# Gathered top bytes moved from a tile of their own into the tile of the joined words

## The chip, the cores and the metric

One Trainium2 chip, one of its cores. The metric is the device time of one execution of the program in microseconds (us); differences are taken between medians of several executions.

## The reference

For 8 batches of 576 rows, the kernel computes linear attention for 8 heads of 64, an RMS norm, and a mixing and feed-forward part. Cut to what matters:

```python
kv  = einsum('bhsd,bhse->bhde', k, v)
out = einsum('bhsd,bhde->bhse', q, kv)
x   = out / sqrt(mean(out * out, axis=-1) + 1e-6) * g_norm   # heads side by side: (8, 576, 512)
u   = x + ((x.T @ U) @ V).T                                  # along the sequence, rank 32
y   = u + maximum(u @ w_ch1, 0) @ w_ch2                      # 512 -> 2048 -> 512
```

All values are float32, except U, V, w_ch1 and w_ch2, which arrive as 64-bit floating-point words and have to be joined to 32-bit words on the chip.

## The kernel before, in words

**Names.** P is 128 partitions, DM is 512, a pair is two heads, a piece f (0 to 15) is 128 columns of w_ch1 with the 128 matching rows of w_ch2, a block j (0 to 8) is 512 rows of the 4608.

**Weights.** `load_w` brings piece f as 64-bit words (1 MB) into a weight slot; SyncE (SP) issues the loads. `decode_w` turns it into float32 and splits it into a high and a low part, `ws`, in the same slot. Piece 0 is decoded in two halves, w1 and w2, by `decode_first`, with parts of the tile `temps` as the target; pieces 1 to 15 take the tile `dec`, of which the pool holds two, so that pieces of equal parity share one. `decode_bytes` has seven steps for a piece:

- line 104, ScalarE (ACT): the gather, byte 4 of every 8-byte word into the tile `packed`, first part (b)
- lines 105, 106, 107 and 109, VectorE (DVE): four operations on these bytes, from b into the second part (c), four bytes to a 32-bit word
- line 111, ACT: c, byte by byte, into the top bytes of the tile `top`
- line 112, DVE: the low words, shifted, are joined with `top` into `temps` or `dec`

Then ACT casts the joined words to the high part (line 117 in `split`, line 125 for the halves), and DVE subtracts it for the low part (line 118, or 137). There is one `packed` and one `top`.

**Attention.** For each batch and pair: `kv_step` (lines 241, 245, and the copies into `kvb`, line 125), `out_step` (lines 264 to 268), `stats_step` (280 to 286), `mul_step` (293, 295), `xsplit_step`, `turn_step`, `t_step` (333, 336), `t4_step` (for the first batch the cast of line 125 on ACT or 131 on DVE, and the subtraction of line 347 on DVE, both into a tile that is called `st` for pairs 1 to 3), and the mix. For the first batch the mix is `mix_first` (matmuls of line 378 before them as fill, 387) and `mix_rest` (396, 398, line 127 into `ut`, then the casts of line 117 into `uth` and the subtractions of line 118 into `utl`).

**Feed-forward.** For each block j and piece f: `ffn1` (lines 414 to 416, three matmuls for each of four column groups), `relu` (line 423 on ACT gives hh, line 424 on DVE gives hl), and `ffn2` of the piece before (line 431). During block 0 `decode_w` runs two pieces ahead; during blocks 0 to 6 the attention of the next batch is woven in.

**Order.** The source is written in the order of a table (`PLAN`); a scheduler that lays the work out by its own estimate then sets the order on each engine, with the tiles' buffers as limits. Each engine works through its own order, and an instruction whose inputs or buffers are not free holds those behind it.

Of the kernel before, what the change touches and what calls it, by code (L numbers as in the profile page):

```python
# [14 lines left out]
U32 = mybir.dt.uint32  # L15
# [5 lines left out]
DM, DF, R = 512, 2048, 32  # L21
P = 128
# [26 lines left out]
def build(ctx: ExitStack, tc: tile.TileContext, kv_in, kvt0_in, kvt_in, q_in, uv_in, g_in, w_in, out):  # L49
# [6 lines left out]
    sc = ctx.enter_context(tc.tile_pool(name="sc", bufs=1))  # L56
    st = ctx.enter_context(tc.tile_pool(name="st", bufs=3))
    dec = ctx.enter_context(tc.tile_pool(name="dec", bufs=2))
    pk = ctx.enter_context(tc.tile_pool(name="pk", bufs=1))
    sm = ctx.enter_context(tc.tile_pool(name="sm", bufs=2))  # L60
    ps_y = ctx.enter_context(tc.tile_pool(name="ps_y", bufs=4, space=bass.MemoryType.PSUM))
    ps_h = ctx.enter_context(tc.tile_pool(name="ps_h", bufs=1, space=bass.MemoryType.PSUM))
# [11 lines left out]
    def weight_slot(name, shape, dtype, f):  # L74

        return const.tile(shape, dtype, name=name, tag=f"w_{f}")
# [18 lines left out]
    def decode_bytes(raw, tmp, top):  # L95

        n = tmp.shape[-1]
        words = raw.bitcast(U32).rearrange("p (n t) -> p n t", t=2)  # L100
        ends = raw.bitcast(U8).rearrange("p (n t) -> p n t", t=8)[:, :, 4]
        packed = pk.tile([P, 2, DM // 2], U32, name="packed")
        b, c = packed[:, 0, 0:n // 4], packed[:, 1, 0:n // 4]
        nc.scalar.copy(out=b.bitcast(U8), in_=ends)
        nc.vector.tensor_scalar(out=c, in0=b, scalar1=0x7f7f7f7f, scalar2=None, op0=ALU.bitwise_and)
        nc.vector.tensor_scalar(out=c.bitcast(U8), in0=c.bitcast(U8), scalar1=56.0, scalar2=71.0, op0=ALU.max, op1=ALU.min)
        nc.vector.tensor_scalar(out=c, in0=c, scalar1=3, scalar2=0x38383838,
                                op0=ALU.logical_shift_left, op1=ALU.bitwise_and)
        nc.vector.scalar_tensor_tensor(out=c, in0=b, scalar=0xC0C0C0C0, in1=c,
                                       op0=ALU.bitwise_and, op1=ALU.bitwise_or)  # L110
        nc.scalar.copy(out=top[:, 0:n].bitcast(U8).rearrange("p (n t) -> p n t", t=4)[:, :, 3], in_=c.bitcast(U8))  # L111
        nc.vector.scalar_tensor_tensor(out=tmp.bitcast(U32), in0=words[:, :, 0], scalar=5, in1=top[:, 0:n],
                                       op0=ALU.logical_shift_right, op1=ALU.bitwise_or)

    def split(hi, lo, src, lo_eng):

        nc.scalar.copy(out=hi, in_=src)
        lo_eng.tensor_tensor(out=lo, in0=src, in1=hi.bitcast(F32), op=ALU.subtract)

    def move(which, n, out, in_, mul=None):  # L120

        e = ENG[which][n]
        if e == "a":
            if mul is None:
                nc.scalar.copy(out=out, in_=in_)
            else:
                nc.scalar.mul(out=out, in_=in_, mul=mul)
        else:
            eng = nc.vector if e == "v" else nc.gpsimd
            if mul is None:  # L130
                eng.tensor_copy(out=out, in_=in_)
            else:
                eng.tensor_scalar(out=out, in0=in_, scalar1=mul, scalar2=None, op0=ALU.mult)

    def minus(which, n, out, in0, in1):
        eng = nc.vector if ENG[which][n] == "v" else nc.gpsimd
        eng.tensor_tensor(out=out, in0=in0, in1=in1, op=ALU.subtract)
# [36 lines left out]
    raws, w1s, w2s = {}, {}, {}  # L174
# [16 lines left out]
    def keep(which, f, hi, lo):  # L191
        w_sb[which][f] = [t.rearrange("p (d c) -> p d c", c=P) for t in (hi, lo)]

    def decode_first(which, tmp, n):
        decode_bytes(raws.pop(which), tmp, tops[n % 1])
        w = const.tile([P, 2, DM], F32R, name=f"{which}s0", tag=f"{which}_0")
        move("wh", n, w[:, 0], tmp)
        minus("wl", n, w[:, 1], tmp, w[:, 0].bitcast(F32))
        keep(which, 0, w[:, 0], w[:, 1])

    def decode_w(f):

        tmp = dec.tile([P, 2 * DM], F32, name="dec")
        decode_bytes(raws.pop(f), tmp, tops[f % 1])
        w = weight_slot(f"ws{f}", [P, 2, 2, DM], F32R, f)
        t = tmp.rearrange("p (w c) -> p w c", w=2)
        split(w[:, 0], w[:, 1], t, nc.vector)
        for n, which in enumerate(("w1", "w2")):
            keep(which, f, w[:, 0, n], w[:, 1, n])
# [245 lines left out]
    tops = [const.tile([P, 2 * DM], U32, name=f"top{n}") for n in range(1)]  # L455
# [73 lines left out]
    for p in range(NPAIR):  # L529
# [5 lines left out]
        tasks.append((PLAN["pair"][p] + PLAN["mt"][p], lambda p=p: mix_rest(p)))  # L535
    ahead = 1
    tasks.append((PLAN["w0"], lambda: decode_first("w1", early[0], 0)))
    tasks.append((PLAN["x0"], lambda: decode_first("w2", early[1], 2)))
    for _, what in sorted(tasks, key=lambda t: t[0]):
        what()  # L540
# [39 lines left out]
    for j in range(NBLK):  # L580
        todo = prep_schedule(j + 1)
        y = None
        for f in range(NF):
            if j == 0:
                while ahead < min(NF, f + 1 + AHEAD):
                    decode_w(ahead)
                    ahead += 1
            end = False
            if j == 0 and f < NEARLY:
                h = hs[f]  # L590
                ffn1(h, f, [3], j)
            else:
                end = j == NBLK - 1 and f == NF - 1
                h = ps_p.tile([P, BLK], F32, name="pp") if end else ps_h.tile([P, BLK], F32, name="h")
                ffn1(h, f, range(ND), j)
            hcur = (f, *relu(h, end))
            for w in todo.get(2 * f, []):
                w()
            if hprev is not None and not (j == NBLK - 1 and f > NF - 3):
                ffn2(y_prev if f == 0 else y, [hprev])  # L600
            if f == 0:
                if j > 0:
                    finish(y_prev, j - 1)
                y = outputs(j)
            for w in todo.get(2 * f + 1, []):
                w()
            held = (held + [hcur])[-3:]
            hprev = hcur
        y_prev = y
# [58 lines left out]
```

## Time and profile before

| | |
|---|---|
| median of 3 executions | 927.5 us (926.78 to 928.56) |
| the profiled execution, its own time | 928.11 us |
| its span, first to last instruction | 926.3 us |
| busy: TensorE (PE), DVE, ACT, POOL | 910.5, 412.2, 281.0, 49.1 us |
| mean granted clock of PE | 0.994 of the full one |
| PE in the first of 40 slices of the span | 7 tenths busy, 9 or more from the third on |

Times in the rows count from the start of the span. A row of the timeline has the start and the length of a record; the brackets behind it say how long the engine was idle before it and what ended that.

### The profile page before, as it was taken

How to read it: one execution, taken by the hardware profiler on the slowest of the kernel's cores; microseconds unless marked ns; L12 is line 12 of the kernel's file. 1: busy time of each engine (PE TensorE's matmuls, PEld its weight loads, DVE VectorE, ACT ScalarE, POOL GpSimd, SP SyncE). 2: the span in 40 equal slices, each digit the busy share in tenths (PEclk: the TensorE clock that was granted, in tenths of full speed). 3: DMA queues.
4: the chain of work that ended last, by engine and by line, in shares of the span. 5: the costliest groups of instructions: out<-in, count | busy, mean ns of one | idle time of the engine just before them, and what ended most of it. 6: DMA issues, size and time to landing. Idle time of an engine off the chain costs nothing.

```text
span 926.3 us, 12207 instructions
## 1 busy us (share of the span) xinstructions
PE 910.5 (98%) x4570; PEld 763.4 (82%) x4570; DVE 412.2 (44%) x885; ACT 281.0 (30%) x587; POOL 49.1 (5%) x68
## 2 busy tenths in 40 slices
PE   7799999999999999999999999999999999999998
PEld 6678888888888888888888888888788888888887
DVE  5988896443354435434344445434344331112112
ACT  5677773222232222222222222222222121111110
POOL 3000002000020002000200010000200020002000
PEclk9899999999999999999999999999999999999999
DMA  9952213121132122212121112212111010001001
GB/s 344 418 217 71 68 57 90 64 68 44 47 101 59 28 77 81 69 32 76 51 61 55 55 57 64 83 31 72 59 49 27 13 46 1 1 1 45 1 1 46
DMA packets 42875, 65.48 MB, mean 71 GB/s; under 512 B 9664, under 2 KB 27840, under 8 KB 42816
## 3 DMA queue, kind: packets, MB, share of 16 engines
q1 hardware_dynamic: 42816, 64.70, 21.2%
q8 instruction: 36, 0.59, 0.3%
q14 instruction: 23, 0.19, 0.1%
HBM read 46.97 MB, written 9.44 MB: 61 GB/s over the span
## 4 chain that ended last, share of the span: by engine, by line
PE 94%; DVE 3%; DMA 1%; ACT 1%; issue 0%; POOL 0%; SPq 0%; DVEq 0%; POOLq 0%
PE y L431 40%; PE h L414 14%; PE h L415 14%; PE h L416 14%; PE pp L241 3%; PE pp L264 3%; PE pp L336 1%; DMA w1raw<-w_in 1%; PE pp L406 1%; PE pp L338 1%; PE pp L266 1%; PE pp L431 1%; DVE utl L372 0%; ACT top L111 0%; DMA out<-st 0%
## 5 line engine op out<-in xcount | busy, mean ns | idle before, releaser
L431 PE MATMUL y<-hh,ws 128*128 128x512 f32 (+1 forms) x1072 | 351.1, 394 | 0.0
L424 DVE SCALAR_TENSOR_TENSOR hl<-h,hh 128x512 fp32r<-128x512 f32 x142 | 97.9, 689 | 301.3 <-ACT hh L423 299.9
L431 PEld LDWEIGHTS y<-hh,ws 128*128 128x128 f32 x1072 | 194.1, 188 | 36.2 <-ACT hh L423 0.6
L414 PE MATMUL h<-uth,ws 128*128 128x512 f32 x536 | 211.7, 395 | 1.3 <-DVE hl L424 1.3
L415 PE MATMUL h<-utl,ws 128*128 128x512 f32 x536 | 210.1, 392 | 0.0
L416 PE MATMUL h<-uth,ws 128*128 128x512 f32 x536 | 209.6, 391 | 0.0
L431 PE MATMUL y<-hl,ws 128*128 128x512 f32 (+1 forms) x536 | 207.2, 387 | 0.0
L423 ACT ACTIVATE hh<-h 128x512 fp32r<-128x512 f32 x142 | 84.8, 597 | 389.9 <-PE h L416 389.6
L414 PEld LDWEIGHTS h<-uth,ws 128*128 128x128 f32 x536 | 101.1, 189 | 24.8 <-DVE hl L424 3.0
L416 PEld LDWEIGHTS h<-uth,ws 128*128 128x128 f32 x536 | 101.1, 189 | 21.9
L431 PEld LDWEIGHTS y<-hl,ws 128*128 128x128 f32 x536 | 100.6, 188 | 20.7
L415 PEld LDWEIGHTS h<-utl,ws 128*128 128x128 f32 x536 | 101.1, 189 | 20.1
L443 POOL TENSOR_TENSOR st<-st,utl 128x512 f32<-128x512 f32 x32 | 40.6, 1290 | 784.7 <-DVE st L442 781.4
L408 DVE TENSOR_TENSOR ut<-pp,ut 128x288 f32<-128x288 f32 x56 | 24.9, 456 | 46.0 <-DMA ut<-xt 32.4
L442 DVE TENSOR_TENSOR st<-y,uth 128x512 f32<-128x512 f32 x32 | 21.3, 686 | 45.7 <-PE y L431 32.1
L371 ACT ACTIVATE uth<-ut,g_sb 128x448 fp32r<-128x448 f32 (+7 forms) x56 | 27.6, 530 | 44.1 <-DVE ut L408 35.1
L280 DVE TENSOR_REDUCE sums<-x 128x10 f32<-128x640 f32 x32 | 26.1, 817 | 24.4 <-ACT x L268 24.4
L372 DVE SCALAR_TENSOR_TENSOR utl<-ut,g_sb,uth 128x448 fp32r<-128x448 f32 (+7 forms) x56 | 26.9, 513 | 11.8 <-ACT uth L371 6.5
L241 PE MATMUL pp<-kv_sb 128*128 128x128 f32 x232 | 31.5, 274 | 0.0
L241 PEld LDWEIGHTS pp<-kv_sb 128*128 128x128 f32 x232 | 29.5, 191 | 1.1
L264 PE MATMUL pp<-kvb,q_sb 128*128 128x128 f32 x224 | 29.5, 274 | 0.0
L264 PEld LDWEIGHTS pp<-kvb,q_sb 128*128 128x128 f32 x224 | 28.3, 191 | 0.8
(202 smaller groups left out, 779.7 us busy)
## 6 DMA issues: line engine op xcount, KB each, us to landing
raw<-w_in SPq DMA_DIRECT2D x15, 1023.6 KB, 14.8
kv_sb<-kv_in SPq DMA_DIRECT2D x29, 512.0 KB, 3.5
q_sb<-q_in SPq DMA_DIRECT2D x29, 288.0 KB, 2.9
out<-st SPq DMA_DIRECT2D x32, 256.0 KB, 2.0
ut<-xt SPq DMA_DIRECT2D x224, 20.0 KB, 1.8
ut<-xt SPq DMA_DIRECT2D x224, 16.0 KB, 1.8
kvt_sb<-kvt_in SPq DMA_DIRECT2D x27, 128.0 KB, 3.1
kvq<-kv_in SPq DMA_DIRECT2D x3, 512.0 KB, 9.4
```

The lines of the kernel that those rows point to most:

```text
L241: nc.tensor.matmul(pp[:, 0:P], lhsT=m[:, i * P:(i + 1) * P], rhs=m[:, MAIN + i * P:MAIN + (i + 1) * P], start=(i == 0 and b < NATIVE), sto ...
L264: nc.tensor.matmul(big[:, i * P:(i + 1) * P], lhsT=qt[:, TAIL + i * P:TAIL + (i + 1) * P], rhs=kb, start=True, stop=True)
L280: nc.vector.tensor_reduce(out=sums.rearrange("p (i h) -> p i h", h=2), in_=xv, axis=AX.X, op=ALU.add)
L371: nc.scalar.mul(out=hi, in_=src, mul=g_sb)
L372: nc.vector.scalar_tensor_tensor(out=lo, in0=src, scalar=g_sb, in1=hi.bitcast(F32), op0=ALU.mult, op1=ALU.subtract)
L414: nc.tensor.matmul(h, lhsT=w1s[f][0][:, d, :], rhs=uh[:, d, :], start=(d == 0), stop=False)
L415: nc.tensor.matmul(h, lhsT=w1s[f][0][:, d, :], rhs=ul[:, d, :], start=False, stop=False)
L416: nc.tensor.matmul(h, lhsT=w1s[f][1][:, d, :], rhs=uh[:, d, :], start=False, stop=(d == ND - 1))
L423: nc.scalar.activation(out=hh, in_=h, func=AF.Relu)
L424: nc.vector.scalar_tensor_tensor(out=hl, in0=h, scalar=0.0, in1=hh.bitcast(F32), op0=ALU.max, op1=ALU.subtract)
L431: nc.tensor.matmul(acc, lhsT=w2s[f][w][:, c, :], rhs=h[:, cols], start=(f == 0 and w == 0 and h is hh), stop=(f == NF - 1 and w == 1))
L443: nc.gpsimd.tensor_tensor(out=o, in0=o, in1=ul[:, c, :].bitcast(F32), op=ALU.add)
```

## The change

The pool `pk` and its tile `packed` are gone. The bytes b and what is made of them, c, now lie in the first and second quarter of `tmp`, the tile that line 112 writes at the end: `temps` for the two halves of piece 0, one of the two `dec` tiles for the others. The two other lines name the one tile `top` directly, and change nothing.

```diff
@@ build
-    pk = ctx.enter_context(tc.tile_pool(name="pk", bufs=1))
@@ decode_bytes
-        packed = pk.tile([P, 2, DM // 2], U32, name="packed")
-        b, c = packed[:, 0, 0:n // 4], packed[:, 1, 0:n // 4]
+        b, c = [tmp[:, i * n // 4:(i + 1) * n // 4].bitcast(U32) for i in range(2)]
@@ decode_first
-        decode_bytes(raws.pop(which), tmp, tops[n % 1])
+        decode_bytes(raws.pop(which), tmp, tops[0])
@@ decode_w
-        decode_bytes(raws.pop(f), tmp, tops[f % 1])
+        decode_bytes(raws.pop(f), tmp, tops[0])
```

The numbers of the later lines fall by two (line 104 of before is line 102 of the change, 112 is 110, 378 is 376). With other buffers the scheduler also lays the instructions out in another order. PE's order is the same up to the first matmuls of line 431; SP's is the same for its first 33 loads. Three places where ACT's and DVE's differ:

ACT, around the cast into `st` for pair 3 of the first batch, before (rawN and wsN belong to piece N):

```order
L127 ACTIVATE ut32_2_94<-y_514,g_sb_97 128x64
L117 CAST uth_569<-ut32_1_93 128x64
L117 CAST uth_569<-ut32_2_94 128x64
L111 COPY top0_103<-packed_547 128x1024
L125 CAST st_141<-y_449 64x128
L104 COPY packed_590<-raw3_174 128x1024
L117 CAST ws2_555<-dec_546 128x1024
```

and in the change:

```order
L115 CAST ws2_548<-dec_540 128x1024
L102 COPY dec_669<-raw4_179 128x1024
L109 COPY top0_100<-dec_582 128x1024
L125 ACTIVATE ut32_0_89<-y_481,g_sb_94 128x64
L125 ACTIVATE ut32_1_90<-y_485,g_sb_94 128x64
L125 ACTIVATE ut32_2_91<-y_509,g_sb_94 128x64
L115 CAST uth_562<-ut32_0_89 128x64
L115 CAST uth_562<-ut32_1_90 128x64
L115 CAST uth_562<-ut32_2_91 128x64
L123 CAST st_138<-y_446 64x128
```

The gather of piece 3, which stood behind the cast into `st`, has moved ahead of these rows, and the gather of piece 4 stands at the top, behind the cast of piece 2 and ahead of everything for pair 3.

DVE, the same place, from the last byte operation of piece 2 to the subtraction into `st`, before:

```order
L109 SCALAR_TENSOR_TENSOR packed_547<-packed_547 128x256
L118 TENSOR_TENSOR utl_570<-ut32_0_92,uth_569 128x64
L118 TENSOR_TENSOR utl_570<-ut32_1_93,uth_569 128x64
L118 TENSOR_TENSOR utl_570<-ut32_2_94,uth_569 128x64
L112 SCALAR_TENSOR_TENSOR dec_546<-raw2_172,top0_103 128x1024
L347 TENSOR_TENSOR st_141<-y_449,st_141 64x128
```

and in the change, from the subtraction that gives the low part of piece 2:

```order
L116 TENSOR_TENSOR ws2_548<-dec_540,ws2_548 128x1024
L105 TENSOR_SCALAR dec_582<-dec_582 128x256
L107 SCALAR_TENSOR_TENSOR dec_582<-dec_582 128x256
L103 TENSOR_SCALAR dec_669<-dec_669 128x256
L104 TENSOR_SCALAR dec_669<-dec_669 128x1024
L110 SCALAR_TENSOR_TENSOR dec_582<-raw3_171,top0_100 128x1024
L105 TENSOR_SCALAR dec_669<-dec_669 128x256
L116 TENSOR_TENSOR utl_563<-ut32_0_89,uth_562 128x64
L116 TENSOR_TENSOR utl_563<-ut32_1_90,uth_562 128x64
L116 TENSOR_TENSOR utl_563<-ut32_2_91,uth_562 128x64
L345 TENSOR_TENSOR st_138<-y_446,st_138 64x128
```

Lines 112 and 118 of piece 2, all five operations of piece 3 and three of piece 4 (dec_669) now stand ahead of the subtraction into `st`; before, line 112 of piece 2 was the last of the decoding ahead of it.

ACT, around the copies into `kvb` for the first pair of batch 1, before:

```order
L104 COPY packed_678<-raw4_182 128x1024
L117 CAST ws3_598<-dec_589 128x1024
L125 COPY kvb0_101<-pp_579 64x64 x2
L423 ACTIVATE hh_561<-pp_524 128x512
L423 ACTIVATE hh_614<-h_601 128x512
```

and in the change:

```order
L115 CAST ws4_677<-dec_669 128x1024
L115 CAST uth_562<-ut32_3_92 128x64
L102 COPY dec_836<-raw6_183 128x1024
L123 COPY kvb0_98<-pp_572 64x64 x2
L109 COPY top0_100<-dec_768 128x1024
L421 ACTIVATE hh_554<-pp_519 128x512
L421 ACTIVATE hh_606<-h_593 128x512
```

The gather ahead of the copies is that of piece 6 rather than piece 4, and the copy into `top` for piece 5 (dec_768) stands between the copies and the first relu.

## Rows read from the trace of the kernel before

**Rows 1.** Busy us, share of the span and count of each engine (the page).

```profile
PE 910.5 (98%) x4570; PEld 763.4 (82%) x4570; DVE 412.2 (44%) x885; ACT 281.0 (30%) x587; POOL 49.1 (5%) x68
```

**Rows 2.** Stretches: length, busy us of each engine, PE's clock, DMA share, GB/s.

```profile
40.00:50.00 10.00, 7.64 (x32) 6.21 (x33) 7.19 (x15) 7.92 (x14) 0.00 (x0) 0.66 1.02 420
...
64.00:160.00 96.00, 96.00 (x504) 81.07 (x503) 78.66 (x153) 60.94 (x102) 4.83 (x4) 1.00 0.23 70
```

**Rows 3.** PE's waits: us in total, times, longest us.

```profile
PE h L378 <- DVE st L347: 3.2, 2, 2.4
```

**Rows 4.** Timeline of PE, 43 to 64 us: start, length, instruction, idle before.

```profile
43.67 1.22 PE L378 MATMUL h<-v,st 128*128 128x512 f32 x2 [2.36 <-DVE st L347]
...
45.75 0.63 PE L415 MATMUL h<-utl,ws 128*128 128x512 f32 x1
...
48.74 0.63 PE L416 MATMUL h<-uth,ws 128*128 128x512 f32 x1
...
52.12 1.05 PE L264 MATMUL pp<-kvb,q_sb 128*128 128x128 f32 x8
...
53.16 1.18 PE L431 MATMUL y<-hh,w2s 128*128 128x512 f32 x4
54.17 0.39 PE L431 MATMUL y<-hl,w2s 128*128 128x512 f32 x1
54.40 0.40 PE L431 MATMUL y<-hh,w2s 128*128 128x512 f32 x1
...
63.02 0.50 PE L414 MATMUL h<-uth,ws 128*128 128x512 f32 x1 [0.51 <-DVE hl L424]
```

**Rows 5.** Timeline of DVE, 21 to 53 us.

```profile
21.41 0.82 DVE L280 TENSOR_REDUCE sums<-x 128x10 f32<-128x640 f32 x1 [0.54 <-ACT x L268]
...
39.73 0.42 DVE L109 SCALAR_TENSOR_TENSOR packed<-packed 128x256 uint32<-128x256 uint32 x1
...
42.07 1.23 DVE L112 SCALAR_TENSOR_TENSOR dec<-raw,top 128x1024 uint32<-128x1024 uint32 x1 [1.01 <-ACT top L111]
43.33 0.28 DVE L347 TENSOR_TENSOR st<-y,st 64x128 fp32r<-64x128 f32 x1
43.64 0.29 DVE L105 TENSOR_SCALAR packed<-packed 128x256 uint32<-128x256 uint32 x1
43.97 0.69 DVE L106 TENSOR_SCALAR packed<-packed 128x1024 uint8<-128x1024 uint8 x1
44.58 1.22 DVE L118 TENSOR_TENSOR ws<-dec,ws 128x1024 fp32r<-128x1024 f32 x1
45.72 0.29 DVE L107 TENSOR_SCALAR packed<-packed 128x256 uint32<-128x256 uint32 x1
46.07 0.75 DVE L390 SCALAR_TENSOR_TENSOR utl<-pp,g_sb,uth 128x512 fp32r<-128x512 f32 x1
46.74 0.42 DVE L109 SCALAR_TENSOR_TENSOR packed<-packed 128x256 uint32<-128x256 uint32 x1
47.07 0.22 DVE L118 TENSOR_TENSOR utl<-ut,uth 128x64 fp32r<-128x64 f32 x1
...
52.49 0.69 DVE L424 SCALAR_TENSOR_TENSOR hl<-pp,hh 128x512 fp32r<-128x512 f32 x1
```

**Rows 6.** Timeline of ACT, 40 to 52 us.

```profile
40.42 0.38 ACT L117 CAST uth<-ut 128x64 fp32r<-128x64 f32 x2
40.71 1.33 ACT L111 COPY top<-packed 128x1024 uint8<-128x1024 uint8 x1
41.91 0.25 ACT L125 CAST st<-y 64x128 fp32r<-64x128 f32 x1
42.07 1.13 ACT L104 COPY packed<-raw 128x1024 uint8<-128x1024 uint8 x1
...
51.19 0.42 ACT L125 COPY kvb<-pp 64x64 f32<-64x64 f32 x2 [0.33 <-PE pp L245]
51.85 0.60 ACT L423 ACTIVATE hh<-pp 128x512 fp32r<-128x512 f32 x1 [0.24 <-PE pp L416]
```

## Prediction

> **What bounds the kernel now.** I read the busy times first. TensorE (PE) is busy for 98% of the span, the next engine for 44% [rows 1]. So a change in the decoding, which is work of ScalarE (ACT) and VectorE (DVE), can only count where PE is not yet fed without a break. The table of stretches says where that is: from 64 to 160 us PE is busy for 96.00 of 96.00 us at the full clock; from 40 to 50 us it is busy for 7.64 of 10 us, at a granted clock of 0.66 [rows 2]. The list of PE's waits names the longest that a decoding step can touch: the matmul of line 378 waits for DVE's line 347, 3.2 us in two waits, the longest of them 2.4 us [rows 3].
>
> The timeline of PE shows that place. At 43.67 us line 378 (the mix of pair 3, the last head pair of the first batch) starts after 2.36 us of idleness, and the feed-forward part begins right behind it [rows 4]. From there to 49.17 us the 128x512 matmuls start 0.427 us apart (7 steps between 45.75 and 48.74), the lower clock level of 1.2 GHz; later they start 0.23 us apart (54.17 and 54.40). At 63.02 us there is one more wait, 0.51 us, for the low part of the hidden layer.
>
> Then DVE and ACT around the long wait. Line 347 needs ACT's cast of line 125 into st, which starts at 41.91 us [rows 6]. But it runs only at 43.33, because line 112 of weight piece 2 stands ahead of it on DVE and waits 1.01 us for ACT's line 111 [rows 5]. So the last wait ends where decoding and attention share two in-order queues; the order of these queues decides.
>
> **The change part by part.** Every instruction stays, with its shape, so I price their durations as unchanged. That the operands lie in another tile could still alter a rate. The nearest evidence is that lines 105 and 107, with different sources and targets inside packed, both take 0.29 us [rows 5]; I take zero. On either side, a tenth on the five DVE decode operations ahead of line 347 would be 0.3 us.
>
> What goes is one wait: the gather of line 104 no longer waits for line 111 of the piece before, which had to read packed first: it starts at 42.07, and line 111 ends at 40.71 + 1.33 = 42.04 us [rows 6]. What comes is another: a gather now writes the dec tile, of which there are two, so the gather of piece f waits until DVE's line 118 of piece f-2 has read it. And the order moves: the gathers and the four byte operations stand up to a piece earlier, on DVE ahead of steps of pair 3. SP's first 33 loads keep their order; pieces land long before use, so I cost the loads at nothing. If they were late, the gather would wait in ACT's queue.
>
> **Step 1, DVE's work ahead.** Up to the end of line 109 of piece 2, DVE of before is at 39.73 + 0.42 = 40.15 us [rows 5]. In the changed order the same work plus lines 112 and 118 of piece 2 and lines 105 and 106 of piece 3 is done when line 118 of piece 2 ends. These take 1.23, 1.22, 0.29 and 0.69 us, and a record starts 0.08 us before the end of an independent one ahead of it (44.58 + 1.22 against 45.72): 3.43 - 4 x 0.08 = 3.1 us. Call that end T. If DVE waits as much on the way as before, T is 43.3; if the 0.54 us wait at 21.41 [rows 5] is wholly filled by decode work that now stands ahead of it, 42.7. I take 42.9, nearer the filled end, since lines 105 and 106 of piece 1 now stand ahead of it.
>
> **Step 2, the new wait.** ACT comes to the gather of piece 4 soon after its cast of piece 2, some 2.4 us before T and waits: that cast needs line 112 of piece 2, and between this and T stand 3.4 us of DVE records (lines 390, 105, 106, 118 and two of pair 3). Queued behind it are line 111 of piece 3, six small casts for the tail columns and the cast into st that PE waits for. From T: gather 42.93 to 44.06 (1.13), line 111 from 43.98 to 45.31 (1.33) [rows 6], DVE's line 112 of piece 3 from 45.35 to 46.58, line 107, three small subtractions of 0.22 us, then line 347 at 47.13 [rows 5]. The cast into st would be done at about 45.3 + 1.1 + 0.25 = 46.7 us (two of the six small casts take 0.38 us together) [rows 6], so DVE's queue decides. PE's line 378 follows 0.34 us later as now (43.33 to 43.67): 47.47 us, **3.8 us later**. With T at its ends, 3.6 to 4.2.
>
> **Step 3, what follows.** PE takes 8.45 us from line 378 to line 264 (43.67 to 52.12) [rows 4], so it would be there at 55.9 us, or at 53.3 if the clock were full all the way (5.5 us shrink by 47%). But line 264 needs the copies into kvb, and these too now stand behind a gather, that of piece 6, which waits for line 118 of piece 4. From 47.13: line 109 to 47.75, line 111 to 49.12, line 112 to 50.39, lines 105, 106, 390, 107 and 118 to 53.35, gather to 54.51, copies (0.42) to 54.85. So line 264 starts between 55.0 and 55.9. Line 431 then needs hh, behind line 111 of piece 5 (56.10, hh to 56.62), and from its fifth matmul on hl, behind line 112 of piece 5 (57.37), line 109 (57.71) and line 424 (58.32) [rows 5, 6]. So the matmul that stands at 54.17 now starts at 58.35: **4.2 us later**, whatever the clock did before it.
>
> **Step 4, what comes back.** The decoding is then at least a piece further on, so I drop the 0.51 us wait at 63.02 [rows 4]. The sum is 4.2 - 0.5 = **+3.7 us**. Behind it PE has no gap that could shrink [rows 2]. A new gap of up to 1 us is possible while pieces 7 to 15 are decoded.
>
> **The clock.** After its 2.36 us gap PE ran at the lower level for 5.5 us [rows 4]; I let the longer gap (2.36 + 3.8 us) be followed by no more than that, which step 3 hides. The Trainium skill ("TensorE: Matmul & The Clock Gate", Part 1: The HAM clock gate) says that the lower rate is the default and that sustained activity releases it, so a longer idleness and the waits of step 3 would leave PE slow for longer. By that rule, with line 264 to the fifth matmul of line 431 also slow, the sum would be about +4.8 us. Without the rule, slow matmuls of lines 264 and 266 (1.04 us now, 52.12 to 53.16, 1.9 then) and four of line 431 at 0.427 us would put that matmul at 55.9 + 1.9 + 1.7 = 59.5 us, 5.3 later; less 0.5 this is +4.8, my upper end before the gap of step 4.
>
> **Against which time.** The profiled execution took 928.1 us, its span 926.3; the sum gives 931.8 on it. It lies 0.6 us above the median of 927.5, so the forecast for the median is **931.2 us**.
>
> **The rivals.** (a) *Faster: the decoding really gets ahead.* If the steps of pair 3 were not pushed back, line 347 could run when st is cast, 41.91 + 0.25 + 0.03 = 42.2 us, 1.1 us earlier; the 0.51 us at 63.02 goes too, and the shorter gap could give back some 1.7 us of the slow stretch (two thirds of 5.5 x 0.47, a guess between none and all). That is -3.3 us, 924.2. It decides if line 118 of piece 2 ends before ACT reaches the gather of piece 4, near 40.4 us. For it speak the waits on line 111 (1.01 us here); against it the 3.1 us of DVE work that stand ahead in the order. The Trainium skill ("Trainium Kernel Development and Optimization", Best Practices) advises double-buffering for performance, and two tiles in place of one is that; no run shown tells yet that it holds here. Chance 0.07.
> (b) *No change: given back.* PE arrives late at line 378, but the full clock returns at 49.17 as before: the slow stretch is 3.8 us shorter, which saves 3.8 x 0.47 = 1.8 us, and if the copies into kvb and hl come early enough not to matter, with 0.5 us at 63.02, what is left is 3.8 - 1.8 - 0.5 = +1.5 us: 929.0. For it speaks the return of the full clock at 49.17 within one stretch of matmuls [rows 4], against it the queues of step 3. Chance 0.13.
> (c) My forecast, with the slow clock of +4.8 and the gap in it: 0.80.
>
> **How the numbers follow.** A difference of 0.2%, 1.9 us, is about what a measurement of this kernel can tell from no change. The forecast's own range is +2.5 to +5.8 us. The range given reaches from case (b) to the top of this: 928.8 to 933.6. Faster by more than 0.2% is case (a), 0.07; within it is case (b) and the low edge of (c), 0.13; slower is the rest, 0.80.
>
> **What would show it.** In the changed profile: ACT idle for about 2.4 us ahead of the gather of line 102, ended by DVE's subtraction; PE's line 376 (378 now) near 47.5 us after a gap of 4 to 6 us; a wait for the copies into kvb near 54 us; no gap of half a microsecond near 63 us of the old count. Wrong would be: PE's mix of pair 3 before 44 us, or a full clock from 47 us on with line 429 already at 56.

## The result, and the profile after

The changed kernel took **933.6 us** (median, 933.0 to 934.4), the kernel before beside it 928.03 us (926.78 to 928.83): ratio 1.0062, interval [1.0044, 1.0079], so 4.1 to 7.3 us slower. The forecast was 931.2 us, 3.7 us slower, with a range up to 933.6: the right sign, 2.4 us too low. The profiled execution took 933.96 us, its span is 932.2 us.

The page of the changed kernel, busy time by engine, against [rows 1]:

```profile
PE 913.3 (98%) x4570; PEld 764.9 (82%) x4570; DVE 410.5 (44%) x885; ACT 280.1 (30%) x587; POOL 49.2 (5%) x68
```

The same 4570 matmuls. Span less busy is 18.9 us (15.8 before): 3.1 us more idle time of TensorE; the other 2.8 us are matmuls that took longer.

Its table of stretches, with the columns of [rows 2]:

```profile
40.00:50.00 10.00, 7.87 (x38) 6.30 (x37) 8.77 (x19) 6.94 (x13) 0.00 (x0) 0.67 1.01 418
64.00:160.00 96.00, 96.00 (x502) 80.72 (x501) 74.78 (x151) 55.85 (x95) 1.72 (x2) 1.00 0.21 62
```

The stretch that I had looked at is no emptier than before (7.87 against 7.64 us). So the new idle time is not all where I expected it. The list of TensorE's waits (us in total, times, longest us) says where, against [rows 3]:

```profile
PE h L376 <- DVE st L345: 3.6, 3, 2.1
PE pp L316 <- DVE x L291: 2.3, 2, 1.5
...
PE pp L331 <- DVE xh L307: 1.8, 1, 1.8
```

Its timeline of TensorE from 15.98 us on, against [rows 4]; at 24.92 us starts the mix of the first pair, pair 0:

```profile
15.98 2.04 PE L316 MATMUL pp<-ident,x 128*128 128x128 f32 x8 [0.81 <-DVE x L291]
...
24.00 1.16 PE L316 MATMUL pp<-ident,x 128*128 128x128 f32 x8 [0.31 <-DVE x L293]
24.92 1.18 PE L376 MATMUL h<-v,t 128*128 128x512 f32 x4
...
37.73 1.13 PE L316 MATMUL pp<-ident,x 128*128 128x128 f32 x8 [1.50 <-DVE x L291]
...
47.84 1.22 PE L376 MATMUL h<-v,st 128*128 128x512 f32 x2 [2.13 <-DVE st L345]
...
52.49 0.63 PE L413 MATMUL h<-utl,ws 128*128 128x512 f32 x1
52.92 0.49 PE L414 MATMUL h<-uth,ws 128*128 128x512 f32 x1
...
57.69 1.23 PE L429 MATMUL y<-hh,w2s 128*128 128x512 f32 x4 [0.27 <-ACT hh L421]
59.27 0.51 PE L429 MATMUL y<-hl,w2s 128*128 128x512 f32 x1 [0.34 <-DVE hl L422]
```

The mix of pair 3 starts at 47.84 us (43.67 before), the first matmul with hl at 59.27 us (54.17 before). The gap ahead of the mix is 2.13 us, no longer than before; but the transposes of pair 3 (line 316), which followed without a gap, now wait 1.50 us. Those ahead of the mix of pair 0 now wait too, 0.31 us. Before, the two places were:

```profile
22.70 1.16 PE L318 MATMUL pp<-ident,x 128*128 128x128 f32 x8
...
34.13 1.84 PE L318 MATMUL pp<-ident,x 128*128 128x128 f32 x8
```

DVE and ACT at that place, the timelines of the changed kernel, against [rows 5, 6]. DVE:

```profile
41.98 1.22 DVE L116 TENSOR_TENSOR ws<-dec,ws 128x1024 fp32r<-128x1024 f32 x1
...
45.64 1.23 DVE L110 SCALAR_TENSOR_TENSOR dec<-raw,top 128x1024 uint32<-128x1024 uint32 x1 [0.23 <-ACT top L109]
...
47.50 0.28 DVE L345 TENSOR_TENSOR st<-y,st 64x128 fp32r<-64x128 f32 x1
...
57.05 1.23 DVE L110 SCALAR_TENSOR_TENSOR dec<-raw,top 128x1024 uint32<-128x1024 uint32 x1 [0.69 <-ACT top L109]
...
58.53 0.68 DVE L422 SCALAR_TENSOR_TENSOR hl<-pp,hh 128x512 fp32r<-128x512 f32 x1
```

ACT:

```profile
43.23 1.12 ACT L102 COPY dec<-raw 128x1024 uint8<-128x1024 uint8 x1 [2.59 <-DVE ws L116]
44.25 1.35 ACT L109 COPY top<-dec 128x1024 uint8<-128x1024 uint8 x1
...
46.49 0.26 ACT L123 CAST st<-y 64x128 fp32r<-64x128 f32 x1
...
53.84 1.13 ACT L102 COPY dec<-raw 128x1024 uint8<-128x1024 uint8 x1 [1.34 <-DVE ws L116]
55.22 0.42 ACT L123 COPY kvb<-pp 64x64 f32<-64x64 f32 x2 [0.24 <-PE pp L243]
```

The operations on the bytes last as long as before (line 102 1.12 us, 109 1.35, 110 1.23), so the new place of the bytes adds nothing to their durations. The chain of steps 2 and 3 is there: the gather of piece 4 waits 2.59 us for the subtraction of piece 2, and joins stand ahead of `st` and of hl on DVE.

**A loss far behind.** One more place stands 220 us later, in the feed-forward part, where nothing is decoded any more. TensorE of the changed kernel:

```profile
266.78 0.40 PE L429 MATMUL y<-hh,w2s 128*128 128x512 f32 x1
267.48 1.19 PE L429 MATMUL y<-hh,ws 128*128 128x512 f32 x4 [0.31 <-ACT hh L421]
268.89 0.50 PE L412 MATMUL h<-uth,ws 128*128 128x512 f32 x1 [0.22 <-DVE hl L422]
```

and of the kernel before:

```profile
260.41 0.39 PE L431 MATMUL y<-hh,w2s 128*128 128x512 f32 x1
260.64 1.09 PE L431 MATMUL y<-hh,ws 128*128 128x512 f32 x4
261.57 0.39 PE L414 MATMUL h<-uth,ws 128*128 128x512 f32 x1
```

The two steps take 0.70 and 1.41 us in place of 0.23 and 0.93: 0.95 us lost. ACT's timeline shows why, after:

```profile
265.45 1.50 ACT L369 ACTIVATE uth<-ut,g_sb 128x192 fp32r<-128x192 f32 x4 [4.93 <-DVE st L440]
266.85 0.57 ACT L421 ACTIVATE hh<-h 128x512 fp32r<-128x512 f32 x1
```

and before:

```profile
258.29 0.60 ACT L423 ACTIVATE hh<-h 128x512 fp32r<-128x512 f32 x1 [0.90 <-PE h L416]
259.82 1.50 ACT L371 ACTIVATE uth<-ut,g_sb 128x192 fp32r<-128x192 f32 x4 [0.93 <-DVE st L442]
```

The scheduler has put four operations for the next block ahead of hh, in code that the change doesn't touch.

**How the profiles are compared below.** The clock of the first 26 us differs from one execution to the next, so times from the start of the span mislead. I cut each span at three starts on TensorE: A is the start of the mix of pair 0 (24.92 us above; the expectations of the last two runs call it the mix of pair 1), B the time from there to the mix of pair 3 (47.84), C from there to the first matmul with hl (59.27), D from there to the end of the span.

| kernel, run | own time | A | B | C | D |
|---|---|---|---|---|---|
| before | 928.11 | 23.61 | 20.06 | 10.50 | 872.1 |
| before, e11_before2 | 931.31 | 27.14 | 19.86 | 10.46 | 872.0 |
| before and 5 fills, e13_bwarm5 | 928.50 | 24.38 | 19.91 | 10.43 | 872.0 |
| changed | 933.96 | 24.92 | 22.92 | 11.43 | 872.9 |
| changed, e5_again | 931.53 | 23.07 | 22.93 | 11.05 | 872.7 |
| changed, e12_after3 | 933.48 | 24.68 | 22.92 | 11.19 | 872.9 |
| changed and 5 fills, e14_awarm5 | 933.18 | 23.74 | 22.91 | 11.21 | 873.5 |
| e6_chain7 (gathers to piece 7 held) | 929.28 | 24.24 | 20.37 | 10.49 | 872.4 |
| e1_chain (all gathers held) | 929.81 | 22.87 | 20.39 | 10.39 | 874.4 |
| e9_hold123 | 934.94 | 27.21 | 20.37 | 11.06 | 874.6 |
| e10_hold4 | 933.37 | 25.09 | 22.95 | 10.66 | 872.9 |
| e4_late5 (before; dec from piece 5) | 928.44 | 24.08 | 19.77 | 9.58 | 873.3 |
| e2_dec3 | 940.59 | 24.53 | 28.14 | 11.97 | 874.2 |
| e3_packed2 | 935.76 | 24.19 | 27.21 | 9.49 | 873.1 |
| e7_afill | 930.18 | 24.76 | 22.98 | 9.32 | 871.3 |
| e8_bfill | 928.27 | 23.56 | 20.19 | 9.49 | 873.3 |

B is the same to 0.2 us in all rows of one order, whatever A is. By means, the changed kernel is longer by 2.98 us in B (22.92 against 19.94), 0.76 in C (11.22, 10.46) and 0.96 in D (873.01, 872.05): **4.7 us** (4.4 by the unaltered executions alone, since D is 0.6 us longer in e14_awarm5 than in them). A depends on the clock, but one piece of it differs at the full clock: from the last start of line 264 (262) ahead of the mix of pair 0 to this mix, 4.55 to 4.56 us in all four rows of the changed kernel (20.36 to 24.92 in the first) against 4.18 before (19.43 to 23.61; the same in e13_bwarm5). Most of these 0.4 us is the wait of 0.3 us ahead of line 316 shown above. In e11_before2 the clock was low there, so that it can't be compared.

### The profile page after: what moved, and what is told of

The parts are those of the page before. It is cut to its first block, busy times and chain, and to the rows that moved or that the text cites. A ratio compares the mean times of both kernels' runs of the same rounds, so it can differ in the third digit from the quotient of the medians.

```text
span 932.2 us, 12221 instructions
## 1 busy us (share of the span) xinstructions
PE 913.3 (98%) x4570; PEld 764.9 (82%) x4570; DVE 410.5 (44%) x885; ACT 280.1 (30%) x587; POOL 49.2 (5%) x68
## 4 chain that ended last, share of the span: by engine, by line
PE 69%; DVE 1%; DMA 0%; POOL 0%; issue 0%; DVEq 0%; POOLq 0%
PE y L429 31%; PE h L412 11%; PE h L413 10%; PE h L414 10%; PE pp L239 2%; PE pp L262 2%; DVE utl L370 1%; PE pp L429 1%; PE pp L334 1%; PE pp L404 0%; PE pp L336 0%; DMA out<-st 0%; DVE st L440 0%; PE pp L264 0%; DVE hl L422 0%; POOL st L441 0%
```

## The experiments

Three theories. **Order**: with two tiles to write to, the scheduler puts gathers and byte operations ahead of attention steps in the in-order queues of ACT and DVE. **Wait**: the gather's new wait for the subtraction of two pieces earlier is what costs. **Place**: the operations are slower on operands in `dec`.

**Order put back, place kept (e1_chain).** In `decode_bytes` of the changed kernel:

```diff
-        nc.scalar.copy(out=b.bitcast(U8), in_=ends)
+        with tc.issue_after(last_top[0].ins) if last_top[0] is not None else nullcontext():
+            nc.scalar.copy(out=b.bitcast(U8), in_=ends)
...
-        nc.scalar.copy(out=top..., in_=c.bitcast(U8))
+        last_top[0] = nc.scalar.copy(out=top..., in_=c.bitcast(U8))
```

> The change, with the bytes still in the tile of the joined words, but each gather is put behind the previous piece's copy into the top tile in ScalarE's order, as the single byte tile forced it before; no wait is added by this. Theory A (order): the change loses because gathers and byte operations move ahead of the attention of pairs 2 and 3 in the queues of ScalarE and VectorE; then most of the loss comes back: 928 to 931 us, pair 3's mix at 43 to 45 us instead of 47.8. Theory B (two tiles): the loss is the wait of a gather for one of two tiles; a gather that comes later finds its tile free more often: also 928 to 931. Theory C (place): the operations are slower where the bytes now lie; nothing comes back: 933 to 934.

Measured: 930.81 us, ratio 1.0031 [1.0019, 1.0042]. B is back at 20.39 us and C at 10.39, with the bytes in `dec`: their place is not what delays the mix. Order and wait this run doesn't part, since a gather that comes later also finds its tile free. What is left is mostly in D, 2.3 us longer than before, with one wait of TensorE (its timeline):

```profile
117.54 1.19 PE L432 MATMUL y<-hh,ws 128*128 128x512 f32 x4 [1.53 <-ACT hh L424]
```

ACT's timeline there:

```profile
114.54 1.36 ACT L112 COPY top<-dec 128x1024 uint8<-128x1024 uint8 x1 [0.67 <-DVE dec L110]
115.76 1.11 ACT L105 COPY dec<-raw 128x1024 uint8<-128x1024 uint8 x1
116.89 0.60 ACT L424 ACTIVATE hh<-h 128x512 fp32r<-128x512 f32 x1
```

A late gather, held behind its copy, now stands ahead of hh.

**More buffers (e2_dec3, e3_packed2).** The changed kernel with three `dec` tiles; the kernel before with two `packed` tiles. In both, `ident` shares a buffer with `xt` and the DMA scratch is 256 instead of 1024, for room; no run has these two alone.

```diff
-    dec = ctx.enter_context(tc.tile_pool(name="dec", bufs=2))
+    dec = ctx.enter_context(tc.tile_pool(name="dec", bufs=3))
```

```diff
-    pk = ctx.enter_context(tc.tile_pool(name="pk", bufs=1))
+    pk = ctx.enter_context(tc.tile_pool(name="pk", bufs=2))
```

> The change with three tiles for the joined words instead of two (half a kilobyte for it comes from the identity matrix sharing a buffer with a later tile, the rest from an unused scratch area). A gather then waits for the piece three before. Theory A (order): the gathers and byte operations can be laid out still further ahead of the attention steps, so it gets no better and likely worse: 933 to 938 us, pair 3's mix at 48 us or later. Theory B (two tiles): the wait of 2.6 us ahead of the gather of piece 4 goes, and with it the loss: 927 to 930 us. Theory C (place): 933 to 934.

> The kernel before, with two byte tiles instead of one (room for it as in the run with three tiles). Bytes lie in tiles of their own, a gather never waits for a tile of the joined words, but it is free to run one piece ahead. Theory A (order): it loses like the change, 931 to 935 us, pair 3's mix after 46 us. Theory B (two tiles) and theory C (place): no loss, 926 to 929 us.

Measured: 940.33 us, 1.0131 [1.0116, 1.0145], and 935.85 us, 1.0088 [1.0075, 1.0101]. A third tile, which loosens the gather's wait, makes B 5.2 us longer still (28.14); a second `packed`, in which no gather waits for a `dec` tile, makes it 7.3 us longer than before (27.21). That speaks against the wait and for the order: the more room, the further ahead the decoding is put. Both times missed my ranges upward, by 2.3 and 0.9 us; what the shared buffer has in this is not shown. Waits of TensorE in e2_dec3:

```profile
PE h L376 <- DVE st L345: 6.1, 2, 3.2
PE pp L316 <- DVE x L291: 3.4, 2, 2.6
```

The Trainium skill ("Trainium Kernel Development and Optimization", Best Practices) advises double-buffering for performance, to overlap DMA with compute. No DMA lands in the byte tiles or in `dec`, so the advice doesn't reach them, and my rival (a) had stretched it; more room made the kernel slower in these two runs and in the change.

**Place alone, later (e4_late5).** The kernel before, with the bytes of pieces 5 to 15 in `dec`:

```diff
+        if piece < 5:
             packed = pk.tile([P, 2, DM // 2], U32, name="packed")
             b, c = packed[:, 0, 0:n // 4], packed[:, 1, 0:n // 4]
+        else:
+            b, c = [tmp[:, i * n // 4:(i + 1) * n // 4].bitcast(U32) for i in range(2)]
```

> The byte tile of before for pieces 0 to 4, the tile of the joined words for pieces 5 to 15. Theory A (order): the order up to the first feed-forward pieces is that of before, so the loss at pair 3's mix (about 4 us) and at the copies into kvb (1 us) is gone; what is left is what the later pieces do to block 0, 0 to 2 us: 927.5 to 930. Theory B (two tiles): the gathers of the later pieces may still wait, but TensorE has work by then: 928 to 930. Theory C (place): 11 of 16 pieces keep the cost, 931 to 932 us.

Measured: 928.7 us, 1.0009 [0.9997, 1.0021]: no difference that can be told. The loss needs the early pieces.

**The unaltered kernels again (e5_again, e11_before2, e12_after3).**

> The changed kernel once more, unaltered, for its time against more runs and for the granted clock in its first 60 us. If the low clock at 15.2 to 18.6 us in its first profile belongs to the change, it is there again at the same place, and the changed kernel's time stays near 933.6 us with the low stretches at 15, 39 and 46 us. If the place at which the clock falls differs from one execution to the next, it falls elsewhere (in the profile before it fell at 32 and at 42 us), the mix of pair 3 begins at 46.5 to 48.5 us all the same, since DVE's line 345 sets it, and the first product with hl begins between 58.0 and 59.5 us, later the longer the clock was low between 46 and 53 us.

> The kernel before, unaltered, for a second profile of it: if the place at which the clock falls in the first 60 us differs between executions, it falls elsewhere than at 32 and 42 us; the mix of pair 3 is at 43 to 45 us all the same, the first matmul with hl at 53.5 to 55.5 us. Time 926 to 930 us.

> The changed kernel, unaltered, for a third profile beside that of the kernel before on the same chip: mix of pair 3 at 46 to 48 us, first matmul with hl at 57 to 59.5 us, 931.5 to 936.5 us; 2 us or more above the lower of these only if the clock was low in a stretch before the mix, as at 15 to 18 us in its first profile.

Measured: the changed kernel 933.79 us over six executions (931.53 to 936.4), 1.0057 [1.0038, 1.0076], and 933.48 us for one; the kernel before 931.31 us for one. The clock's fall belongs to neither kernel: it is there between 14 and 18 us in one of the two profiles of the kernel before and in two of the three of the changed one. In e5_again the low clock at 15 us is not there, and its line 316 takes 1.13 us in place of 2.04 (timeline of TensorE):

```profile
15.56 1.13 PE L316 MATMUL pp<-ident,x 128*128 128x128 f32 x8 [0.81 <-DVE x L291]
```

In e11_before2, the kernel *before*, TensorE runs low for most of 14 to 26 us (stretches, the clock is the third number from the end):

```profile
14.00:18.00 4.00, 3.40 (x19) 3.13 (x20) 3.62 (x8) 2.82 (x7) 2.81 (x7) 0.61 1.04 406
18.00:22.00 4.00, 4.00 (x19) 3.47 (x19) 2.12 (x8) 0.57 (x3) 0.00 (x0) 0.50 1.02 423
22.00:26.00 4.00, 4.00 (x27) 3.88 (x26) 1.99 (x5) 2.59 (x7) 0.00 (x0) 0.61 1.01 409
```

Its A is 3.53 us longer, and at the end its own time is 3.20 us longer: what is lost early is hardly given back. My expectations of the starts missed: the mix of e11_before2 at 47.00 us, its first matmul with hl at 57.46 and its time above my ranges, those of e5_again (46.00 and 57.05) below, since I had taken starts from the beginning of the span. By B, 19.86 and 22.93, the two agree with the other rows of their order.

In e12_after3 the gap ahead of the mix is longer than in the other profiles of the unaltered kernels, and the low clock behind it (0.427 us from one matmul to the next) ends at 52.24 us:

```profile
47.60 1.22 PE L376 MATMUL h<-v,st 128*128 128x512 f32 x2 [3.64 <-DVE st L345]
...
51.82 0.63 PE L412 MATMUL h<-uth,ws 128*128 128x512 f32 x1
52.24 0.46 PE L413 MATMUL h<-utl,ws 128*128 128x512 f32 x1
```

**Only the early gathers held (e6_chain7).** As e1_chain, for the pieces up to 7 alone:

```diff
-        decode_bytes(raws.pop(f), tmp, tops[0])
+        decode_bytes(raws.pop(f), tmp, tops[0], f > 7)
```

> The changed kernel with the gathers of the pieces up to 7 alone held back until the top copy of the piece before is issued; the later ones are free as in the changed kernel. Theory A (order): the loss at pair 3 stays away as in e1_chain (mix near 43.3 us), and the wait of 1.5 us at 117.5 us, which I put down to a late gather that was held back and then stood ahead of an hh copy, goes: 928 to 930 us, ratio 1.000 to 1.002. Rival: what e1_chain was slower than the kernel before (3 us) comes from the place of the bytes or from the joined tile, and then it stays: 930 to 932 us.

Measured: 928.45 us, 1.0006 [0.9996, 1.0016]. The kernel with the change's tiles and this order can't be told from the kernel before: by the interval at most 1.5 of the 5.6 us are left, so most of the loss, and perhaps all of it, is order. B is 20.37 us, 0.4 longer than before. In D, TensorE is busy 340.00 of 340 us between 160 and 500 us (339.48 in the changed kernel): the far wait at 267 us is gone too.

**Which gather (e9_hold123, e10_hold4).** As e6_chain7, with the gathers of w2 and pieces 1 to 3 held, and with that of piece 4 alone.

```diff
-        decode_bytes(raws.pop(f), tmp, tops[0], f > 7)
+        decode_bytes(raws.pop(f), tmp, tops[0], f not in (1, 2, 3))
```

> The changed kernel with the gathers of w2 and pieces 1 to 3 held back until the top copy of the piece before is issued; that of piece 4 and all later ones are free. Order theory: it is the byte operations and joins of pieces 2 and 3, ahead of pair 3's steps in DVE's queue, that make the mix late. Then the mix of pair 3 is back at 43 to 44.5 us; the copy into top and the join of piece 4 now stand ahead of the first hh and hl, so that 0 to 2 us stay there: 928 to 930.5 us. Rival: the wait of piece 4's gather for the subtraction of piece 2 (2.6 us on ACT in the changed kernel) is the cause by itself: it is still there, the mix is at 46 to 48 us and the time 932 to 935 us.

> The changed kernel with the gather of piece 4 alone held back until the top copy of piece 3 is issued; all others are free. The gather of piece 4 then stands behind that copy on ACT, still ahead of the cast into st, and the join of piece 3 still stands ahead of the subtraction into st on DVE. Order theory: the mix of pair 3 stays at 45.5 to 48 us, the time at 931 to 935 us. Rival (the wait of piece 4's gather by itself): the mix is back at 43 to 44.5 us and the time at 927.5 to 930 us.

Measured: 931.67 us, 1.0049 [1.0030, 1.0068], and 933.0 us, 1.0057 [1.0041, 1.0074]. With pieces 1 to 3 held, B is back (20.37). The mix is at 47.58 us, which read from the start of the span would speak for the rival; A is 27.21 here. The time missed my range by 1.2 us: C and D kept more than I allowed (11.06, 874.6). The run doesn't settle the rival, though: the scheduler put the gather of piece 4 behind the cast into `st`, so that its wait was not there ahead of the mix. e10_hold4 does. There the first thing that ACT waits for is the copy into `top` of piece 3 (ACT's timeline):

```profile
44.13 1.35 ACT L112 COPY top<-dec 128x1024 uint8<-128x1024 uint8 x1 [3.31 <-DVE dec L110]
45.35 1.11 ACT L105 COPY dec<-raw 128x1024 uint8<-128x1024 uint8 x1
```

The gather no longer waits, ACT does as long as before (3.31 us, 2.59 in the changed kernel), and B stays at 22.95 (the mix is at 48.04 us, just above my range). So the gather's wait is a place where lateness shows and not its cause by itself. The cause is the free order of w2 and pieces 1 to 3, as e9_hold123 shows; that it acts through DVE's queue, with pieces 2 and 3 ahead of pair 3, is read from the rows and not tested apart.

**Fills for the clock (e7_afill, e8_bfill).** Eight more matmuls into a spare bank ahead of pair 3's transposes, in the changed kernel and in the kernel before (`fill3` 2 to 10):

```diff
-        for _ in range(n):
-            nc.tensor.matmul(spare, lhsT=state[0, p]["t4"], ...)
+        for i in range(n):
+            nc.tensor.matmul(spare, lhsT=state[0, p if p < 3 or i >= 8 else 2]["t4"], ...)
```

> The changed kernel with eight more products into the spare bank, of pair 2's t4, ahead of pair 3's transposes (2 us at the high clock, 4 at the low one); they add work and leave nothing out. They fill the 1.5 us that TensorE was idle before the transposes at 37.73 us. Clock theory: part of the 5.9 us is products at the low clock (39.1 to 42.5 and 45.9 to 52.7 us), so that with the clock kept up the kernel comes to 929 to 932 us. Order theory alone: the mix of pair 3 is set by DVE and ACT, not by TensorE, so that it stays at 47 to 48 us and the time at 932.5 to 936 us, with the fills' own 2 us added if they come too late.

> The kernel before with the same eight products at the same place. There TensorE had no idle time before the transposes at 34.13 us, so the eight cost 2 to 4 us there and take it from the idle 2.36 us before the mix of pair 3 at 43.67 us, if TensorE's own work isn't what that mix waits for. Clock theory: less low clock at 42.4 to 49.2 us, 925.5 to 928 us, faster than both kernels. Rival: the transposes come later by the eight, and DVE and ACT behind them, so that the mix moves to 45.5 us or so and the time to 929 to 931 us.

Measured: 927.46 us, 1.0007 [0.9989, 1.0026], and 928.27 us, 0.9997 [0.9985, 1.0009]. Neither beats the kernel before, and neither time lies in a range of its two theories. In e7_afill B stays long (22.98), as the order theory has it, and yet the loss is gone, in C (9.32) and D (871.3). So a late mix need not cost the kernel its time, and how this run makes it up is not shown. It doesn't tell clock from order: its ACT queue changed too, the copy into `top` of piece 5 standing behind the first hh instead of ahead of it. In e8_bfill the clock was high from 22 to 42 us and C a microsecond shorter (9.49), but D 1.2 us longer.

**A busier start (e13_bwarm5, e14_awarm5).** Five products of `ident` with itself around the first `kv_step`, in the kernel before and in the changed one:

```diff
+    def early_fill(p, n):
+        t = ident if p == 0 else kvb[0]
+        for _ in range(n):
+            nc.tensor.matmul(spare[:, 0:P], lhsT=t, rhs=t, start=True, stop=True)
...
+        if p < 2:
+            tasks.append((PLAN["pair"][p] + PLAN["out"][p], lambda p=p: early_fill(p, (5, 0)[p])))
```

> The kernel before with five more products of the identity with itself into the spare bank, two ahead of the first kv_step and three behind it, in the 2.6 us that TensorE is idle before the first matmuls of line 264; nothing is left out, the order of all else stays. In the profiles so far the mix of pair 1 starts between 22.9 and 27.2 us, the later the longer the clock was low between 10 and 26 us, in kernels of either order. If a busier start keeps the clock up, the mix of pair 1 is at 23 to 24 us in the profile and the times lie closer together: 926 to 928 us, ratio 0.998 to 1.000. If the fall of the clock has nothing to do with this gap, the times spread as before, 926 to 931 us, ratio 1.000.

> The changed kernel with the same five products at the same place, beside the one of the kernel before on the same chip. From the mix of pair 1 on, three profiles of the changed kernel are 4.3 to 4.6 us longer than two of the kernel before, while the medians lie 5.6 to 6.2 us apart. If the rest (1 to 2 us) is the granted clock of the first 25 us, which falls differently often in the two, and the fill evens that out, this kernel is 4 to 5 us slower than the other of this pair (930.5 to 932.5 us). If the rest is from the order, as the 4.4 us are, the two stay 5.5 to 6.5 us apart (932.5 to 934.5 us).

Measured: 928.14 us, 0.9995 [0.9983, 1.0007], and 933.18 us, 1.0058 [1.0045, 1.0071]. The fills don't reliably keep the clock up: line 318 at 15.60 us takes 2.08 us in e13_bwarm5, while in e14_awarm5 the clock was 1.00 there. The times of e13_bwarm5 lie closer together than those of the kernel before (925.94 to 928.9 in 11 executions, 925.98 to 931.39 in 15); whether the fills do that is not shown. The two are 5.0 us apart, between the two expectations, so the pair doesn't decide. The 4.7 us of the table are near it, and lie within the intervals of both comparisons of the unaltered kernels (4.1 to 7.3 and 3.5 to 7.0 us).

## Why the prediction was right in sign and short in size

- **Place at zero, loads at nothing.** Right: durations as before, and e4_late5 and e6_chain7 lose nothing that can be told.
- **Step 1 and step 2.** T came at 41.98 + 1.22 = 43.20 us (42.9 forecast), ACT waited 2.59 us (2.4), line 345 started at 47.50 (47.13), the mix at 47.84 (47.47). Part of this agreement is luck: A was 1.31 us longer in that execution. By B the mix is 2.98 us later, not 3.8. I also had the lateness in one gap of 4 to 6 us ahead of the mix, which was 2.13 us in the first profile and 3.64 in e12_after3; it came in pieces, 1.50 us of it ahead of pair 3's transposes, as pieces 1 to 3 also push back the steps of pair 2. And I made the wait of piece 4's gather the cause; e10_hold4 shows it isn't, by itself. A had no term: the 0.4 us there I had not seen.
- **Step 3.** The first matmul with hl is later by B and C together, 2.98 + 0.76 = 3.74 us; I had 3.8 + 0.4 = 4.2. As forecast, the copies into `kvb` stand behind a gather (55.22) and hl behind the join of piece 5 (58.53); but line 262 does not wait for the copies, as I had it near 54 us. C differs little with the clock high or low (11.05 to 11.43).
- **Step 4, which failed.** "Behind it PE has no gap that could shrink", and the 0.51 us at 63.02 dropped: the sum went from 4.2 to 3.7. The wait did go; no gap of that kind is in the changed kernel's row from 64 to 160 us, and the matmuls from 62.13 to 64.85 follow without one. But D is 0.96 us *longer*, not 0.5 shorter. 0.95 us stand at 267 us, by an order that I had not compared beyond the decoding; the further half microsecond I can't place on one wait. Step 4 was mis-sized by 1.5 us: -0.5 forecast, +0.96 measured.
- **The clock.** A longer low stretch behind the mix, on which my +4.8 us rested, did not come. From the start of the mix TensorE ran at the lower level for 5.50 us before (43.67 to 49.17), for 5.08 us in the first profile of the changed kernel (47.84 to 52.92), and for 4.64 us in e12_after3, whose gap was the longest (3.64 us). The Trainium skill ("TensorE: Matmul & The Clock Gate", Part 1: The HAM clock gate) says that the throttled clock is the default and that activity releases it; that TensorE stays slow for longer after longer idleness was my own step from it, and these rows don't show it. That +4.8 us came near the size is luck. The early fall at 15.98 us, which I didn't have at all, counts more for a single execution: A spans 23.07 to 27.14 us in unaltered kernels. From 50 to 54 us the clock was 0.61 in the first profile and 0.94 in e5_again, and C is 11.43 and 11.05.
- **The account.** Of the 2.4 us: 0.5 is the kernel before, 928.03 in the comparison, 927.5 in my base; -0.5 steps 1 to 3; 1.5 step 4; and 0.9 is the measured difference of 5.57 less the 4.7 of the three stretches, which lies inside its interval. Of this 0.9, 0.4 stands ahead of the mix of pair 0, at the new wait there; whether the rest is the clock of the first 26 us falling differently often in the two kernels stays open.
- **The range.** Its upper end doesn't follow from my sum: 927.5 + 5.8 is 933.3 us, not 933.6, and (b) with its +1.5 is 929.0, not 928.8.
- **The rivals.** (a), faster, fell: the decoding did get ahead (its last join starts at 118.66 us, 136.01 before), and that was the cost. (b), given back, fell: behind the mix only the wait at 63.02 us came back, and more was lost there than that.

## What to carry to other kernels

A buffer that frees a step of a side job lets a scheduler put that job ahead of steps that the critical path needs, in in-order queues; ask which instructions move ahead of what, then tie the side job down by an explicit order rather than by the want of a buffer (e6_chain7). Compare the order of the whole program, since a changed early part reorders late ones. And compare profiles between two events behind the part in which the clock varies, not from the start of the span.

## What I had not expected of the hardware

The granted clock of TensorE fell at different places in the first 26 us of different executions of one kernel: 1.00 in all three stretches from 14 to 26 us in the profile before, 0.61, 0.50 and 0.61 in e11_before2, which ended 3.20 us later. Most of the time lost there stays lost: in e11_before2 TensorE is busy 340.00 of 340 us from 160 to 500 us, and has hardly a gap to make it up in. A few more matmuls in the first idle stretch didn't prevent it in e13_bwarm5 (0.70 from 14 to 18 us).
